# Attention and two feed-forward layers: the first layer's last two blocks by Strassen's algorithm, attention's weights turned in one piece

## The chip, the cores and the metric

The kernel runs on one core of one Trainium2 chip. The metric is the device time of one execution in microseconds. Before the change the median of three runs is 1072.8 us (1071.49 to 1074.07).

## The reference

Three steps follow one another. `q`, `k` and `v` have 4 batches, 8 heads, 768 positions and 64 channels; the output of attention is laid out as 3072 tokens of 512 channels and goes through two feed-forward layers of the same sizes (512 to 2048 to 512).

```python
for c in range(nc):                          # 24 chunks of 32 positions
    k_ctx = k[:, :, max(0, c*32 - 16):min(S, c*32 + 40)]      # v_ctx alike
    k_full = np.concatenate([mem_k, k_ctx], axis=2)           # 8 memory rows
    scores = scale * np.matmul(q_c, k_full.transpose(0, 1, 3, 2))
    a = np.exp(scores - np.max(scores, axis=-1, keepdims=True))
    a = a / (np.sum(a, axis=-1, keepdims=True) + 1e-09)
    out[:, :, c*32:c*32 + 32] = np.matmul(a, v_full)
x = out.transpose(0, 2, 1, 3).reshape(3072, 512)
h = x @ w_in1;  x = np.maximum(0.01 * h, h) @ w_out1          # layer 1
h = x @ w_in2;  x = (h * np.clip(h + 3, 0, 6) / 6) @ w_out2   # layer 2
```

## The kernel before

**Numbers.** A float32 operand of a product is split into a high part, a cast, and a low part, the operand less that cast; a product is then three matmuls (high by high, high by low, low by high) that add up in one bank. ScalarE makes the casts (`high` L902, `cw_high` L884), VectorE or GpSimd the differences (`low` L906, `cw_low` L888).

**Attention.** Two chunks of 32 positions make a "pair" of 64 tokens; there are 48 pairs, 8 to a block of 512 tokens. From pair 16 on (block 2) two pairs go through together, as a double. TensorE makes the scores of one double and the values of the double before in one visit (`visit` L604); VectorE masks and takes the maxima, ScalarE the exponentials, GpSimd the sums and the scaling. VectorE then turns the weights (`a_turn` L541) in blocks of 32x256, twelve to a double, because the value product wants them with the context along the partitions.

**First layer.** Six blocks of 512 tokens, each by 16 units of 128 of the 2048 hidden channels (`hidden` L723 and `output` L748, both through `mm3` L717; their matmuls stand at L719). The weights of this layer are float64 words that are converted once and stay in the core's memory. The attention of a later block lies between the units of an earlier one.

**Second layer.** The blocks go through in three pairs. For a pair of blocks Strassen's scheme (in Winograd's form) replaces eight products of halves by seven: `PROD, LETTERS, FINAL = 7, "BAEBEBD", "ABEAEAD"` (L777) names, product by product, the banks in which the seven products of the hidden half and of the output half add up, and `WIDE` the buffer that holds the split moving operand of each. All of this layer's matmuls stand at L909. Sums on VectorE stand at L899 (operands, `mix`) and L935 (results, `summed`). The weights of this layer are converted piece by piece while the first layer runs (`combine` L1052; `w_clip` L290, `w_join` L297, the quarter sums L840 and L846), stored to DRAM as seven combinations, and loaded into the place of the first layer's weights when that has ended (`cw_load`). The gated hidden values go to DRAM (`g_store`) and come back for the output half (`g_load`), where the split operands use three buffers in turn (`SPIN`: `xwa`, `xwb`, `fb`).

**Order.** The kernel describes every step with an engine, a duration, a due time and what it needs; `Program.order` (L79) runs these steps through a small model of the engines, taking on each free engine the ready step that is due first, and the instructions are then written out in that order. Each engine works through its own list in order. SyncE issues nearly all transfers.

```python
STEP_FIRST = 6.3
STEP_MIXED = 6.6
STEP = 5.5
rings = dict(w=NF - 3, wb=3, raw=2, wa=1, ye=4, g=2, x=4, py=4, ph=2, pa0=1, pa1=1, qk=1, v=1)
def a_turn(pr, part):
    ...
```

Of the kernel before, what the change touches and what calls it, by code (L numbers as in the profile page):

```python
# [23 lines left out]
    visit=1.45, visit2=2.1, scores=0.75, masked=0.56, most=0.55, exp=0.37, exp_all=0.52, small=0.15, inverse=0.18, norm=0.83, turn=0.6, turned=0.57, turn_two=1.35, masked_two=1.1, most_two=0.97,  # L24
# [3 lines left out]
AFTER = 0.1  # L28
LANDING, RATE = 2.1, 290e3
# [4 lines left out]
STEP_MIXED = 6.6  # L34
STEP = 5.5
# [5 lines left out]
LATER = 35.0  # L41


class Program:
# [34 lines left out]
    def order(self, filler):  # L79
# [14 lines left out]
        free_at = {e: 0.0 for e in ready}  # L94
        pipe, out, left, now = 0.0, [], len(steps), 0.0
# [14 lines left out]
        while left:  # L110
            later = []
            for e in free_at:
# [18 lines left out]
                eng, length, _, fn, args, _, takes, nbytes = steps[best]  # L131
                ready[e].discard(best)
# [28 lines left out]
def tile_kernel(  # L161
# [41 lines left out]
    NPB = TB // PT  # L203

# [6 lines left out]

    y_dram = dr.tile([P, KD, NT], F32, tag="yd", name="y_dram")
    w_dram = [dr.tile([P, 7 * NF // 2, 256], F32, tag=f"wd{io}", name=f"w_dram{io}") for io in range(2)]
    g_dram = [dr.tile([P, NB // 2, NF // 2, TB], F32, tag=f"gd{c}", name=f"g_dram{c}") for c in range(4)]
# [5 lines left out]
    aT_all = at.tile([W, 2, HP, P], F32, tag="aT", name="aT_all")  # L220
# [36 lines left out]
    def w_load(layer, f):  # L257
        n = 1 if layer == 0 and f in (0, NF) else 2
        if layer:
            st, src = raw_pair(0).bitcast(U32), (w_in2, w_out2)[f[0]][2 * f[1]:2 * f[1] + 2]  # L260
# [7 lines left out]
    def w_upper(key):  # L268

        raw = raw_t[key][:, :, :, 1].bitcast(F32)  # L270
        if key[0]:
            a = rows(4).bitcast(U32)
# [108 lines left out]
    def barred_by_pe(pr):  # L381
        return pr < 2 * NPB and 0 < pr % PPB < PPB - 1
# [81 lines left out]

    def a_norm_two(pr, k):
# [75 lines left out]
    def a_turn(pr, part):  # L541

        e, t = both(pr), aT_all.rearrange("p k h c -> p (k h) c")
        r = slice(32 * part, 32 * part + 32)
        for j in range(W // 32):
            c = slice(32 * j, 32 * j + 32)
            nc.vector.transpose(out=t[c, :, r], in_=e[r, :, c])  # L547
        if part == P // 32 - 1:
            aT_t[pr], aT_t[pr + 1] = aT_all[:, 0], aT_all[:, 1]
# [8 lines left out]
    def a_turned(pr):  # L558
        t = aT_all[:, pr % 2]
        nc.scalar.copy(out=t.rearrange("p h c -> p (h c)"), in_=aT_t[pr][:W, :])  # L560
# [787 lines left out]
```

## Time and profile before

| | |
|---|---|
| median of three runs | 1072.8 us |
| profiled execution, its own time | 1073.48 us |
| its span in the profile | 1071.7 us |
| TensorE busy | 1058.7 us (99%) |
| VectorE busy | 741.6 us (69%) |
| ScalarE busy | 557.0 us (52%) |
| GpSimd busy | 131.2 us (12%) |
| moved by transfers | 158.35 MB, 148 GB/s over the span |

The span runs from the first to the last instruction of the profiled execution; the execution's own time is 1.8 us longer. "Busy" of TensorE is modelled from the matmuls' ends, so a busy TensorE may still not be at its best pace. The granted clock is 1.00 in every stage read here. The stages, by the products in them: a lead-in to about 33 us, the first layer to about 610 us, the second layer to the end, in it three hidden halves of 76 us to about 834 us and three output halves after that. The busy share of an engine is an average over these; what a change is worth is read stage by stage.

### The profile page before, as it was taken

The numbers are of one execution on the slowest core, as the hardware profiler recorded it, in microseconds if no ns is written. First come the engines' busy times: TensorE is split into PE (matmuls) and PEld (weight loads), VectorE is DVE, ScalarE is ACT, GpSimd is POOL, SyncE is SP. The second block draws the span as 40 slices with busy tenths as digits, with TensorE's granted clock in tenths as the row PEclk, the third lists the DMA queues.
The fourth block names the chain that finished last, engine by engine and source line by source line (L and its number), as shares of the span: only waits on it lengthen the run. The fifth ranks groups of instructions, "written<-read, shape, count | busy, mean of one in ns | idle before, by whom it ended". The sixth has DMA issues, their size and how long they took to land.

```text
span 1071.7 us, 16147 instructions
## 1 busy us (share of the span) xinstructions
PE 1058.7 (99%) x6107; PEld 871.1 (81%) x6107; DVE 741.6 (69%) x1110; ACT 557.0 (52%) x1083; POOL 131.2 (12%) x159
## 2 busy tenths in 40 slices
PE   8999999999999999999999999999999999999997
PEld 7787888888888888888888888888888888888885
DVE  6999856677667766767433666866855796687684
ACT  6887654343435544434344555656677644444442
POOL 4111101100000010000000001111365400000000
PEclk9999999999999999999999999999999999999999
DMA  9564433343345444433433433433677657257313
GB/s 292 194 213 142 158 130 114 113 153 113 128 136 205 138 147 167 139 128 108 155 93 93 140 149 116 154 143 117 207 224 229 229 139 222 49 158 197 64 54 59
DMA packets 101406, 158.35 MB, mean 148 GB/s; under 512 B 32208, under 2 KB 54736, under 8 KB 101328
## 3 DMA queue, kind: packets, MB, share of 16 engines
q1 hardware_dynamic: 101328, 157.32, 45.7%
q8 instruction: 48, 0.79, 0.3%
q14 instruction: 30, 0.25, 0.1%
HBM read 104.86 MB, written 52.43 MB: 147 GB/s over the span
## 4 chain that ended last, share of the span: by engine, by line
PE 95%; DMA 2%; DVE 1%; ACT 1%; SPq 0%; issue 0%; DVEq 0%
PE ph L719 25%; PE py L719 25%; PE sA L909 12%; PE sE L909 12%; PE sB L909 12%; PE sD L909 6%; PE px L568 2%; PE psc L404 2%; DMA in<-in_v_dram 1%; DMA f<-in_moe_w_dram 1%; DMA cw<-w_dram 1%; PE psc L568 0%; PE pt L555 0%; SPq L369 0%; DVE a L304 0%
## 5 line engine op out<-in xcount | busy, mean ns | idle before, releaser
L719 PE MATMUL py<-g,w 128*128 128x512 f32 x1152 | 279.5, 390 | 0.0
L719 PE MATMUL ph<-xh,w 128*128 128x512 f32 x768 | 258.4, 394 | 0.7 <-ACT xh L584 0.7
L719 PEld LDWEIGHTS py<-g,w 128*128 128x128 f32 x1152 | 215.2, 188 | 45.0 <-DVE g L746 0.2
L719 PEld LDWEIGHTS ph<-xh,w 128*128 128x128 f32 x768 | 144.9, 189 | 31.9 <-ACT xh L584 0.9
L737 ACT ACTIVATE ph<-ph 128x512 f32<-128x512 f32 x96 | 56.0, 583 | 189.6 <-PE ph L719 185.3
L719 PE MATMUL ph<-xl,w 128*128 128x512 f32 x384 | 150.3, 391 | 0.0
L746 DVE TENSOR_TENSOR g<-ph,g 128x512 fp32r<-128x512 f32 x96 | 66.2, 689 | 96.3 <-ACT g L741 95.7
L547 DVE STREAM_TRANSPOSE aT_all<-raw 32x256 f32<-32x256 f32 x192 | 83.4, 435 | 4.5 <-POOL raw L468 1.8
L719 PEld LDWEIGHTS ph<-xl,w 128*128 128x128 f32 x384 | 72.5, 189 | 14.7 <-DVE xl L590 0.3
L945 POOL TENSOR_TENSOR gated<-gated,gated 128x512 f32<-128x512 f32 x24 | 33.8, 1419 | 245.7 <-PE sB L909 130.1
L741 ACT CAST g<-ph 128x512 fp32r<-128x512 f32 x96 | 56.4, 588 | 2.9
L909 PE MATMUL sE<-xwb,cw 128*128 128x512 f32 x240 | 57.6, 389 | 0.0
L531 POOL TENSOR_SCALAR su<-su 128x4 f32<-128x4 f32 (+1 forms) x32 | 9.9, 309 | 368.7 <-ACT raw L461 331.5
L909 PEld LDWEIGHTS sE<-xwb,cw 128*128 128x128 f32 x240 | 45.0, 188 | 9.4
L584 ACT CAST xh<-px 128x512 fp32r<-128x512 f32 (+1 forms) x25 | 12.8, 512 | 71.5 <-PE px L568 71.5
L461 ACT ACTIVATE raw<-raw,mx 128x96 f32<-128x96 f32 x128 | 46.2, 365 | 3.3 <-DVE mx L457 3.3
L909 PE MATMUL sB<-fb,cw 128*128 128x512 f32 x192 | 46.6, 390 | 0.4 <-DVE gated L942 0.4
L909 PE MATMUL sB<-xwa,cw 128*128 128x512 f32 x192 | 46.1, 389 | 0.0
L935 DVE TENSOR_TENSOR sE<-sE,small_ye 128x512 f32<-128x512 f32 x24 | 16.8, 698 | 38.8 <-PE sE L909 38.2
L909 PEld LDWEIGHTS sB<-fb,cw 128*128 128x128 f32 x192 | 36.0, 188 | 8.3 <-DVE gated L942 0.8
L909 PEld LDWEIGHTS sB<-xwa,cw 128*128 128x128 f32 x192 | 36.0, 188 | 7.5
L888 POOL TENSOR_TENSOR cw<-cw 128x512 fp32r<-128x512 f32 x28 | 37.9, 1364 | 33.8 <-ACT cw L884 29.4
(158 smaller groups left out, 1853.8 us busy)
## 6 DMA issues: line engine op xcount, KB each, us to landing
g_dram<-gated SPq DMA_DIRECT2D x96, 256.0 KB, 2.0
f<-in_moe_w_dram SPq DMA_DIRECT2D x15, 1024.0 KB, 5.0
cw<-w_dram SPq DMA_DIRECT2D x56, 256.0 KB, 3.1
raw<-g_dram SPq DMA_DIRECT2D x24, 512.0 KB, 4.0
raw<-in_moe_w_in_dram SPq DMA_DIRECT2D x8, 1024.0 KB, 5.8
w_dram<-raw SPq DMA_DIRECT2D x32, 256.0 KB, 2.3
raw<-in_moe_w_out_dram SPq DMA_DIRECT2D x8, 1024.0 KB, 5.2
qk_now<-in_qk_dram SPq DMA_DIRECT2D x24, 320.0 KB, 4.1
```

The source lines that it names most:

```text
L404: nc.tensor.matmul(pt[j][n * PT:(n + 1) * PT, m * W:(m + 1) * W], qt[r, hp, :], kt[r, hp, :], start=not more, stop=True, tile_position=(e ...
L461: nc.scalar.activation(out=e[:, k, :], in_=e[:, k, :], func=AF.Exp, bias=m_t[pr][:, k:k + 1], accum_out=s_t[pr][:, k:k + 1],)
L547: nc.vector.transpose(out=t[c, :, r], in_=e[r, :, c])
L568: nc.tensor.matmul(pt[e * D:(e + 1) * D, at + hp * every:at + hp * every + PT], vt[:, c], t[:, hp, n * PT:(n + 1) * PT], start=True, stop= ...
L719: nc.tensor.matmul(dst, a, b, start=first and i == 0, stop=last and i == len(terms) - 1)
L737: nc.scalar.activation(out=ph, in_=ph, func=AF.Prelu, alpha=0.01)
L741: nc.scalar.copy(out=g[:, 0, :], in_=ph_t[key])
L746: nc.vector.tensor_sub(out=g[:, 1, :], in0=ph, in1=g[:, 0, :].bitcast(F32))
L888: eng.tensor_tensor(out=w[:, :, 1, :], in0=w[:, :, 1, :].bitcast(F32), in1=w[:, :, 0, :].bitcast(F32), op=ALU.subtract)
L909: nc.tensor.matmul(dst, a, b, start=start, stop=True, skip_group_check=True)
L935: nc.vector.tensor_tensor(out=t if out else b, in0=b, in1=t, op=ALU.add)
L945: nc.gpsimd.tensor_tensor(out=gated(a), in0=gated(b), in1=gated(a), op=ALU.subtract)
```

## The change

The first four blocks of the first layer stay as they were. Its last two go through the same seven-product scheme as the second layer's pairs. For that the attention of these two blocks is written to DRAM (`x_staged`, `x_store`) and loaded back as operands. The first layer's weights, which are held as high and low parts, are added up again (`c_whole`), combined in quarters like the second layer's, and stored; the seven combinations are then streamed back in units of four blocks and split again on VectorE. The hidden values pass a leaky rectifier on ScalarE alone (`rectify`), and the results go to `y_dram`. From here on this stretch is the inserted pair.

Attention of blocks 2 to 5 is packed between the products of blocks 1 to 3. Its weights are turned by one instruction for a double, in 32x32 blocks in place, and the blocks are brought to their partitions by a store to DRAM and three loads. The value products stand two visits behind the scores.

```diff
-    def a_turn(pr, part):
+    def a_turn(pr):
 
-        e, t = both(pr), aT_all.rearrange("p k h c -> p (k h) c")
-        r = slice(32 * part, 32 * part + 32)
-        for j in range(W // 32):
-            c = slice(32 * j, 32 * j + 32)
-            nc.vector.transpose(out=t[c, :, r], in_=e[r, :, c])
...
+        nc.vector.transpose(out=turned_t, in_=both(pr).rearrange("p h (j c) -> p j h c", c=32))
+
+    def turn_store(pr):
+        nc.sync.dma_start(out=turn_dram[pr // 2 % 2], in_=turned_t.rearrange("p j h c -> p j (h c)"))
+
+    def turn_load(pr, j):
+        nc.sync.dma_start(
+            out=aT_all[32 * j:32 * j + 32].rearrange("i r h c -> i r (h c)"),
+            in_=turn_dram[pr // 2 % 2].rearrange("(r i) j x -> i r j x", i=32)[:, :, j, :],
+        )
...
-                    pt[e * D:(e + 1) * D, at + hp * every:at + hp * every + PT], vt[:, c], t[:, hp, n * PT:(n + 1) * PT],
+                    pt[e * D:(e + 1) * D, at + hp * every:at + hp * every + PT].rearrange("p (r c) -> p r c", c=32),
+                    vt[:, c], t[:, 2 * n:2 * n + 2, hp, :],
...
+    def c_whole(key, e):
...
+        w = wt[0, 2 * p + e, io]
+        nc.vector.tensor_tensor(out=rows(4)[:, e, :], in0=w[:, 0, :].bitcast(F32), in1=w[:, 1, :].bitcast(F32), op=ALU.add)
...
-    def cw_load(io, t):
-        nc.sync.dma_start(out=combined(t)[:, :, 1, :].bitcast(F32), in_=w_dram[io][:, 2 * t:2 * t + 2, :])
+    def cw_load(y, io, u):
+        nc.sync.dma_start(out=combined(y, io, u)[:, :, 1, :].bitcast(F32), in_=w_dram[y][io][:, 4 * u:4 * u + 4, :])
...
+    def rectify(letter, k, n):
+        nc.scalar.activation(out=gated(n), in_=sums(letter, k), func=AF.Prelu, alpha=0.01)
...
+    def y_store(blk, c, n):
+        nc.sync.dma_start(out=y_dram[:, c, blk * TB:(blk + 1) * TB], in_=small(n))
...
-    for blk in range(NB):
+    for blk in range(CB):
         block_at[0, blk] = t
-        length[0, blk] = STEP if blk == NB - 1 else STEP_MIXED if blk else STEP_FIRST
+        length[0, blk] = STEP_MIXED if blk else STEP_FIRST
         t += NF * length[0, blk]
...
-    first = block_at[0, 1] + 25
-    every = (block_at[0, NB - 1] - 25 - first) / 16
+    first, end = block_at[0, 1] + 6, hidden_at[0, 0] - 30
     for n in range(16):
-        combine(n % 8, n // 8, first + n * every)
+        combine_first(n % 8, n // 8, first + n * (end - first) / 16)
+    stages = [first, hidden_at[0, 0], output_at[0, 0], *(hidden_at[1, s] for s in range(NS)), output_at[1, 0] - 25]
+    for n, t, u in zip((W0, W1, W2, W3, W4, 16 - W0 - W1 - W2 - W3 - W4), stages, stages[1:]):
+        combine_between(n, t, u)
...
-    WIDE = ["fb8", "x0", "x1", "xwa", "xwb", "x2", "x3"]
-    SPIN = ["xwa", "xwb", "fb8"]
+    WIDE = [["fb8", "x0", "x1", "xwa", "xwb", "x2", "x3"], ["x0", "x1", "xwa", "xwb", "fb8", "x2", "x3"]]
+    SPIN = ["fb8", "xwa", "xwb"]
...
+        if y == 0:
+            cell("ACT", T["relu"], t, rectify, letter, k, n, reads=b, writes=g, **gated_own(n))
+            return n
...
+        for u in range(UNITS):
+            add_weights(y, 1, u, output_at[y, 0] + u * 4 * H6 - 20, "POOL" if y else "DVE")
```

With `CLASSICAL = 4` there are four blocks in the loop over `CB`. `W0` to `W4` (9, 1, 0, 1, 3, and 2 left over) say in which stage the sixteen conversions of second-layer weights lie: nine beside the first layer's blocks, one in the hidden half of the inserted pair, six in the second layer's hidden halves.

**How the order moves.** The rows below are an engine's instructions as they stand one after the other; they hold no times. Names with a number at their end are buffers: `fb8`, `xwa`, `xwb` the split operands, `ob` and `ot` reloaded hidden values, `cw` combined weights, `cv` and `cva` the second layer's weights in conversion.

VectorE in an output half, from the end of the second product on, before (the second layer's first output half):

```order
L906 TENSOR_TENSOR xwb_5587<-ob1_7223,xwb_5587 128x1024
L906 TENSOR_TENSOR fb8_4949<-ot0_7226,fb8_4949 128x1024
L899 TENSOR_TENSOR ot0_7226<-ot0_7226,raw1_1554 128x1024
L899 TENSOR_TENSOR ob0_7115<-ob0_7115,ot0_7226 128x1024
L906 TENSOR_TENSOR xwa_5542<-ot0_7226,xwa_5542 128x1024
L935 TENSOR_TENSOR wa_1834<-sB0_5523,wa_1834 128x512
```

and in the output half of the inserted pair:

```order
L330 ISA cva_1702<-cv_1642,cva_1702 128x2048
L1030 TENSOR_TENSOR fb8_4414<-ob1_0_5072,fb8_4414 128x1024
L956 TENSOR_TENSOR cv_1642<-cva_1702 128x256
L962 TENSOR_TENSOR cv_1642<-cva_1702 128x256
L962 TENSOR_TENSOR cv_1642<-cv_1642,cva_1702 128x256
L962 TENSOR_TENSOR cv_1642<-cva_1702,cv_1642 128x256
L1030 TENSOR_TENSOR xwb_4542<-ot0_0_5076,xwb_4542 128x1024
L1022 TENSOR_TENSOR ot0_0_5076<-ot0_0_5076,raw1_1543 128x1024
L1022 TENSOR_TENSOR ob0_0_4970<-ob0_0_4970,ot0_0_5076 128x1024
L1005 TENSOR_TENSOR cw1_10_5108<-cw1_10_5108 128x4x256
L1030 TENSOR_TENSOR xwa_4529<-ob1_0_5072,xwa_4529 128x1024
```

The split of `ot0` now stands ahead of the last split of `ob1`, a conversion of second-layer weights lies between the splits, and so does a split of combined weights (`cw1_10`), which GpSimd made before.

TensorE at the same place, before (from the last rows of the second product on):

```order
L909 MATMUL sB0_5523<-xwb_5587,cw3_5139 128x512 x3
L909 MATMUL sB1_5535<-xwb_5587,cw3_5139 128x512 x3
...
L909 MATMUL sE0_5593<-fb8_4949,cw4_5175 128x512 x3
L909 MATMUL sE1_5607<-fb8_4949,cw4_5175 128x512 x3
...
```

and in the inserted pair:

```order
L1033 MATMUL sB0_4462<-fb8_4414,cw1_3_4755 128x512 x3
L1033 MATMUL sB1_4475<-fb8_4414,cw1_3_4755 128x512 x3
...
L1033 MATMUL sE0_4522<-xwb_4542,cw1_4_4791 128x512 x3
L1033 MATMUL sE1_4533<-xwb_4542,cw1_4_4791 128x512 x3
...
L1033 MATMUL sB0_4462<-xwa_4529,cw1_3_4755 128x512 x3
L1033 MATMUL sB1_4475<-xwa_4529,cw1_3_4755 128x512 x3
...
```

The first four products of E (from `xwb`) have moved ahead of the last four of B (from `xwa`).

VectorE around the first product of the second layer, before:

```order
L746 TENSOR_TENSOR g0_5_15_5519<-ph0_5_15_5487,g0_5_15_5519 128x512
L906 TENSOR_TENSOR xwa_5542<-raw1_1554,xwa_5542 128x1024
L899 TENSOR_TENSOR raw1_1554<-raw0_1774,raw1_1554 128x1024
L935 TENSOR_TENSOR sA0_5546<-sA0_5546,wa_1834 128x512
L762 COPY yo5_0_5574<-py0_5_0_5005 128x512
```

and now:

```order
L1060 TENSOR_TENSOR small_ye2_4628<-sD0_4545,small_ye2_4628 128x512
L1022 TENSOR_TENSOR raw0_1658<-raw1_1543,raw0_1658 128x1024
L1060 TENSOR_TENSOR small_ye3_4638<-sD1_4589,small_ye3_4638 128x512
L312 TENSOR_SCALAR cva_1702<-cva_1702 128x1024
L1060 TENSOR_TENSOR sA0_4497<-sA0_4497,wa_1644 128x512
L1030 TENSOR_TENSOR xwa_4529<-raw0_1658,xwa_4529 128x1024
L1022 TENSOR_TENSOR raw0_1658<-raw0_1658 128x1024
L1022 TENSOR_TENSOR raw1_1543<-raw1_1543,raw0_1658 128x1024
L1060 TENSOR_TENSOR sA1_4510<-sA1_4510,wa_1644 128x512
L1030 TENSOR_TENSOR xwb_4542<-raw0_1658,xwb_4542 128x1024
```

The last result sums of the inserted pair and the sums of operands and of the next hidden values now stand in one row ahead of `xwa` and `xwb`, with a conversion step (L312) among them.

## Rows read from the trace of the kernel before

**Rows 1.** The page: busy time, share of the span, instructions of each engine.

```profile
PE 1058.7 (99%) x6107; PEld 871.1 (81%) x6107; DVE 741.6 (69%) x1110; ACT 557.0 (52%) x1083; POOL 131.2 (12%) x159
```

**Rows 2.** The page: the chain that ended last, by engine.

```profile
PE 95%; DMA 2%; DVE 1%; ACT 1%; SPq 0%; issue 0%; DVEq 0%
```

**Rows 3.** Waits of TensorE from 33 us on: us in total, times, longest.

```profile
PE ph L719 <- ACT xh L584: 0.7, 1, 0.7
PE sB L909 <- DVE gated L942: 0.4, 1, 0.4
```

**Rows 4.** Windows: from, to, length, then busy time (instructions) of each engine.

```profile
core 0: us, PE busy (x) PEld busy (x) DVE busy (x) ACT busy (x) POOL busy (x), PEclk, DMA share, GB/s
...
134.00:520.00 386.00, 386.00 (x2549) 317.58 (x2549) 262.49 (x481) 169.84 (x442) 32.61 (x48) 1.00 0.41 139
...
760.00:830.00 70.00, 69.64 (x308) 57.30 (x307) 43.87 (x62) 50.14 (x85) 40.69 (x30) 1.00 0.72 232
772.00:776.00 4.00, 4.00 (x20) 3.30 (x19) 1.78 (x3) 2.46 (x6) 2.33 (x2) 1.00 0.97 359
776.00:780.00 4.00, 3.63 (x16) 2.70 (x15) 3.84 (x8) 3.45 (x6) 1.44 (x2) 1.00 0.99 352
912.00:988.00 76.00, 76.00 (x337) 62.94 (x336) 56.56 (x57) 33.68 (x36) 0.00 (x0) 1.00 0.51 139
```

**Rows 5.** Windows, line 719 on TensorE alone: the first layer's products.

```profile
33.00:1072.00 1039.00, 533.93 (x2304) 1.00 0.45 144
```

**Rows 6.** Windows, line 909 on TensorE alone: the second layer's products.

```profile
570.00:1072.00 502.00, 457.62 (x2016) 1.00 0.47 145
```

**Rows 7.** Timeline of TensorE in the last products: start, length, instruction, count.

```profile
1053.20 2.88 PE L909 MATMUL sD<-fb,cw 128*128 128x512 f32 x12
1055.92 2.88 PE L909 MATMUL sD<-xwa,cw 128*128 128x512 f32 x12
```

**Rows 8.** Timeline of TensorE over one attention visit.

```profile
42.38 0.56 PE L404 MATMUL psc<-qk_now 64*64 64x96 f32 x16
42.87 0.69 PE L568 MATMUL psc<-aT_all,v_now 96*64 96x64 f32 x16
43.48 0.73 PE L719 MATMUL py<-g,w 128*128 128x512 f32 x2
```

**Rows 9.** Timeline of VectorE in an output half, instructions back to back.

```profile
1023.72 1.22 DVE L906 TENSOR_TENSOR xwb<-ot,xwb 128x1024 fp32r<-128x1024 f32 x1
1024.85 1.21 DVE L906 TENSOR_TENSOR fb<-ot,fb 128x1024 fp32r<-128x1024 f32 x1
1025.99 1.22 DVE L899 TENSOR_TENSOR ob<-ob,ot 128x1024 f32<-128x1024 f32 x1
```

**Rows 10.** Timeline of ScalarE there: a cast that waited for a buffer.

```profile
1039.80 1.05 ACT L902 CAST fb<-ot 128x1024 fp32r<-128x1024 f32 x1 [1.67 <-PE sE L909]
```

**Rows 11.** Groups of VectorE by form: count, busy, mean ns, idle before.

```profile
L547 DVE STREAM_TRANSPOSE aT_all<-raw 32x256 f32<-32x256 f32 x192 | 83.4, 435 | 4.5 <-POOL raw L468 1.8
L297 DVE SCALAR_TENSOR_TENSOR wa<-raw,wa 128x1024 uint32<-128x1024 uint32 x16 | 19.5, 1220 | 0.4
L935 DVE TENSOR_TENSOR sE<-sE,small_ye 128x512 f32<-128x512 f32 x24 | 16.8, 698 | 38.8 <-PE sE L909 38.2 <-issue 0.6
L290 DVE TENSOR_SCALAR wa<-wa 128x1024 uint32<-128x1024 uint32 x16 | 11.6, 725 | 0.5
L955 DVE STREAM_TRANSPOSE gated<-small_ye 128x512 f32<-128x512 f32 x12 | 7.8, 685 | 0.0
L846 DVE TENSOR_TENSOR raw<-raw,wa 128x256 f32<-128x256 f32 x16 | 7.3, 454 | 0.4
```

**Rows 12.** Timeline of VectorE over one double: masking, then half its turns.

```profile
249.46 1.02 DVE L438 SCALAR_TENSOR_TENSOR raw<-psc,masks 128x384 f32<-128x384 f32 x2 [1.39 <-PE psc L404]
259.42 2.67 DVE L547 STREAM_TRANSPOSE aT_all<-raw 32x256 f32<-32x256 f32 x6
```

More of the change, by code (lines that the diff above doesn't have):

```diff
@@ L40 @@
 COLD = 5.5
-LATER = 35.0
+LATER = 10.0
+CLASSICAL = 4
+LATEST = 0.0
+W0 = 9
+W1 = 1
+W2 = 0
+W3 = 1
+W4 = 3
+PACE = 17.5
+LAST_STEP = 13.0
+SPREAD = 3.4
+BY_ACT = 0
+DEEP = 1
 class Program:
@@ new lines, in sums_of @@
+    def sums_of(key, u, m, w, **more):
+        y, (io, p) = key
+        cell("DVE", T["quarter"], u - 1, c_first, key, reads=[w], writes=[m])
+        for n in range(3):
+            c = cell("DVE", T["quarter"], u - 0.5 + 0.5 * n, c_more, key, n, reads=[w], writes=[m])
+        c_stored[y, io, p] = []
+        for n in range(4):
+            c_stored[y, io, p].append(
+                cell("SP", T["load"], u + 1.5 + 0.5 * n, c_store, key, n, reads=[m] if n > 1 else [w],
+                     nbytes=P * (1024 if n == 1 - io else 2048), **more)
+            )
@@ new lines, in combine_first @@
+    def combine_first(p, io, u):
+        key, m, w = (0, (io, p)), ("raw", 2), ("wide", 0)
+        hold = [max((x for x in paced if x[0] <= u - 10))[1]]
+        u += LATER
+        for e in range(2):
+            f = 2 * p + e
+            cell("DVE", T["sum"], u - 2.5 + 0.7 * e, c_whole, key, e, after=[w_ready[0, f, io], *hold], writes=[w],
+                 takes=takes_early(), frees=[(tag_of(f), ("u", f))])
+        sums_of(key, u, m, w)
+        early.extend(c_stored[0, io, p])
+    taken_early = []
@@ L1102, in wide_own @@
             used[c] = True
-            return dict(takes=[("wb" if c == "xwb" else "w", c)])
-        return own("x", c)
+            return dict(takes=[("wb", c)])
+        return own("x", f"{c}_{y}")
     def bank_own(letter, k):
@@ new lines, in tile_kernel, with add_weights @@
+    SPIN = ["fb8", "xwa", "xwb"]
+    UNITS = PROD * NQ // 4
+    def add_weights(y, io, u, need, eng):
+        stage = ("L", 0) if y else ("S", io)
+        w = [("cw", stage, u)]
+        pairs = {n // PROD if io == 0 else n % NQ for n in range(4 * u, 4 * u + 4)}
+        owned = own(cw_tag(y, u), ("cw", stage, u))
+        taken["w"] = cell("SP", T["load"], need - 24, cw_load, y, io, u, writes=w, nbytes=P * 4096,
+                           **merged(owned, dict(after=[x for p in sorted(pairs) for x in c_stored[y, io, p]] + [taken.get("w")])))
+        cell("ACT", T["wide_copy"], need - 9, cw_high, y, io, u, writes=w)
+        if eng == "DVE":
+            cell("DVE", T["wide"], need - 8, cw_low, y, io, u, nc.vector, writes=w)
+        else:
+            cell("POOL", 2 * T["pool"], need - 8, cw_low, y, io, u, nc.gpsimd, writes=w)
@@ L1219, in load, with mixed @@
                     if dst[0] == "x":
-                        more = own("x", f"o{dst[1]}{w // 2}")
-                    cell("SP", T["load"], due, g_load, c, s, w, dst, writes=[dst], nbytes=P * 4096,
-                         **merged(more, dict(after=[g_stored[c, s, 2 * w + e] for e in range(2)])))
-                def mixed(dst, x, y, op):
-                    cell("DVE", T["wide"], need - 5.4, mix, dst, x, y, op, reads=[x, y], writes=[dst])
+                        more = own("x", f"o{dst[2]}{w // 2}_{y}")
+                    taken["x"] = cell("SP", T["load"], due, g_load, y, c, s, w, dst, writes=[dst], nbytes=P * 4096,
+                         **merged(more, dict(after=[g_stored[y, c, s, 2 * w + e] for e in range(2)])))
+                def mixed(dst, x, z, op):
+                    cell("DVE", T["wide"], need - 5.4, mix, dst, x, z, op, reads=[x, z], writes=[dst])
                 c = SPIN[spun[0] % 3]
```

511 lines of the change are left out of this document (311 added, 200 removed).

## The prediction, made before the changed kernel had run

> **What bounds the kernel now.** I read four views in this order. The page's busy line comes first: TensorE is busy 1058.7 us of 1071.7 us, and VectorE, the next, 741.6 us [rows 1]. A share alone can mislead, so the chain of work that ended last comes second: 95% of it is TensorE [rows 2]. Third, the waits of TensorE after the lead-in: two in 1039 us, 0.7 and 0.4 us [rows 3]. Fourth, the stages: from 134 to 520 us TensorE is busy 386.00 of 386.00 us while VectorE has 262 us of work, and in an output half of the second layer it is busy 76.00 of 76 us beside 56.6 us of VectorE [rows 4]. So only two things move the end: the number of products on TensorE, and a wait that a slower helper puts in front of one.
>
> A product is a matmul of 128x128 by 512 columns. Twelve of them start 2.72 us after the twelve before [rows 7], so one costs 0.2267 us, whatever the 0.39 us in which the profile draws each. That pitch is the price I use, not the busy time.
>
> **The change part by part.**
>
> *Products.* The first layer has 2304 products [rows 5], 384 for each of its six blocks of 512 tokens; two blocks are 768, or 174.1 us. The second layer has 2016 [rows 6], 672 for each pair of blocks, by the same seven-product scheme that the last pair of the first layer now gets: 152.3 us. The difference, 96 products at 0.2267 us, is **-21.8 us**, all of it on the path. I call the new 152.3 us the inserted pair: its hidden half ends at T1, its output half at T2, 76.2 us each.
>
> *Attention on TensorE.* Scores, turns and values are as many as before; they are packed into three blocks instead of four. Sixteen score matmuls start 0.49 us before the next sort, sixteen value matmuls 0.61 us [rows 8]. New is that a value matmul reads its 64 columns in two runs of 32. No row shows that. Below, it cannot gain: the columns are the same. Above, I let a second run cost what separates the two sorts, 0.0075 us, for 768 matmuls: 5.8 us. The time of a matmul here does not follow its columns (96 take less than 64), so I take 0.
>
> *Attention on VectorE.* 192 small transposes, 83.4 us, go [rows 11]. Sixteen of 768 columns come; the nearest rows are 0.435 us for 256 columns and 0.685 us for 512, so about 0.93 us each, 15 us. None of the 68 us saved is on the path, since TensorE lost nothing there [rows 4]; it pays for the new weight sums. What is late next is the road through DRAM: one store and three loads of 128 KB. From the masking to the transposes a double of pairs now takes 10 us [rows 12]; with the turn and two trips of some 3 us that is 17 us. The value products stand two visits behind the scores. Sixteen visits share three blocks, 261 us of products, so two visits are over 32 us. The products between hide it: 0.
>
> *Weights of the first layer.* Thirty-two sums that rebuild a unit, 64 quarter sums and 28 splits of 1024 columns are new on VectorE. In blocks two to four VectorE's rows come to some 68 us per block by the durations before, while a block's products alone take 87 us; the stretch from 134 to 520 us has 262 us in 386 now [rows 4], the same share or a little less. Cost 0; without the products over it, it would be all of those 60 us.
>
> *Output half of the inserted pair.* Here VectorE is closest to the limit. Between T1 and T2 its order holds 27 splits of a moving operand, 13 sums, 11 splits of weights, 8 result sums and one conversion of second-layer weights. Back-to-back instructions of 1024 columns start 1.135 us apart, though each lasts 1.22 us [rows 9]: 51 x 1.135 = 57.9. The result sums are 8 x 0.69 = 5.5, the conversion 2 x 0.72 + 2 x 1.22 + 4 x 0.44 = 5.6 [rows 11]. Together 69 of 76 us, against 56.6 before. An in-order queue this full waits somewhere, and the order shows where. Three buffers hold the split operand, so a split starts when the product three back has ended, plus 0.2 us and a cast of 1.06 us on ScalarE [rows 10]. The sixth split starts at T1 + 3 x 2.72 + 1.3 = 9.4; the conversion's first four rows stand behind it, so the seventh starts at 14.1; the quarter sums and the wait for its buffer put the split of ot0 at 17.6; two sums and cw1_10 follow, so xwa from ob1 starts at 22.15 and is done at 23.4. TensorE, which takes E before the last B, wants it after eight products, at 21.8. It waits **1.7 us**. Later splits meet their product with 0.1 us or more to spare in the same count. Bounds: 0, if loads let the order run ahead, and 8 us, if half of the 15 us more work that this half has than one before lands on TensorE.
>
> *Start of the second layer.* In the old kernel it stands behind products that need few splits. Now VectorE reaches T2 with the last result sums still to do. By its order: sum, mix, sum, shift, then sA0 (which needs TensorE's third unit, T2 + 4.3), then xwa, done at 6.1. TensorE has put five units of 1.36 us before it, 6.8. xwb is done at 10.1 against 10.9. So 0, with 0.7 us to spare. Bounds 0 and 3 us (both splits late by a conversion step of 1.2 us).
>
> *Hand-overs.* Three are new: into the inserted pair, from its hidden to its output half (same tokens, so stored values come back at once), and out of it. The only such place now cost 0.4 us [rows 3, 4]. 3 x 0.4 = **1.2 us**; bounds 0 and 6.
>
> *Six conversions* move into the second layer's hidden halves. A bank is wanted again 4.1 us after its last product, and sum, gate and second gate need about 2.4; one instruction of 1.14 us in front still fits. 0; at most 6 x 1.1 us.
>
> *Lead-in.* Its loads come in another order; I take 0, within 1 us either way.
>
> **Sum.** The profiled execution took 1073.5 us (span 1071.7). 1073.5 - 21.8 + 1.7 + 1.2 = 1054.6 us. The median of the runs, 1072.8, lies 0.7 us lower: **1054 us**.
>
> **Rivals.**
>
> *Transfers bind the inserted pair.* From its first store to the second layer's last row load SyncE issues 106 transfers: stored and reloaded values 16.8 MB, weights 13.6, rows of x and y 6.8, conversions 5.9, together 43.1 MB in 152.3 us, 283 GB/s. For it: from 760 to 830 us the rate was 232 GB/s at a share of 0.72. Against it: that stretch was not full, and full ones reach 352 to 359 GB/s at 0.97 to 0.99 [rows 4]. At 232 GB/s the pair would take 185.8 us, and the time would be 1054 + 33.5 = 1087 us. It turns slower than before when the rate falls below 43.1 / (152.3 + 18.9), 252 GB/s. The Trainium skill (DMA: Bandwidth & Descriptors, section Bandwidth) speaks for this rival: it asks for transfers of 1 MiB and lists 138 GB/s at 64 KB and 341 at 1 MB; between them I estimate some 265 GB/s for transfers of 256 and 512 KB, and the time by that would be about 1064 us. The rows of 352 to 359 GB/s were reached with transfers of 256 and 512 KB, several at once, and they decide. Chance 0.10, of which 0.03 past the turning point.
>
> *VectorE binds the output half.* If the instructions do not overlap (1.22 instead of 1.135 us), its 51 long ones cost 4.3 us more, the half no longer fits with its waits, and those 4.3 us reach TensorE: 1058 us. For it: mixed neighbours on several buffers, and splits that come 0.1 us ahead of their product. Against it: rows 9 are the same instructions. The Trainium skill (VectorE: DVE Perf Modes, section The DRAIN you can't avoid) says the next operation does not start before the pipe is empty, which would be this case; the trace does not agree, with starts 1.13 us apart for operations of 1.22 us. Chance 0.13.
>
> *The turned weights come late (slower).* If the road through DRAM outlasts two visits, TensorE stands still at every one of 16 value visits. From 1.2 us each the saving of 18.9 us is gone; at 2 us it is 1054 + 32 = 1086 us. For it: the transfers stand in SyncE's one queue behind stores that wait for VectorE. Against it: 17 us of work in over 32. Chance 0.07, half of it past the turning point.
>
> **How the numbers follow.** The forecast has 0.70. Its own edges are 1050 (no wait and a lead-in 1 us shorter) and 1060 (5.8 us for the column runs). To leave at most 2 in 10 outside I take in VectorE's case, the mild part of the transfers, and 12 us, nearly half, of the upper bounds above (6.3 + 3 + 4.8 + 5.8 + 6.6 = 26.5 us beyond the values taken): 1050 to 1066. Within 0.2% of before, 2.1 us, counts as no change; that is about what a measurement of this kernel can tell. Slower: 0.03 + 0.03; no change 0.02 between; faster 0.92.
>
> **What would show it.** Right: 4224 products at 0.2267 us; blocks two to four with no wait of TensorE; VectorE near 69 of 76 us in the output half, and one wait of 1 to 2 us on a split into xwa early in it. Wrong: a stretch of the inserted pair with the transfers' share near 1 and TensorE waiting for loads; value products waiting for aT_all; or a wait of over 2 us behind the first xwa of the second layer.

## The result, and the profile after

The changed kernel takes 1055.09 us (median of four runs, 1054.41 to 1055.60) against 1072.14 us of the kernel before in the same comparison: a ratio of 0.9839, 95% interval 0.9828 to 0.9851. The forecast was 1054 us with a range of 1050 to 1066. The profiled execution took 1054.41 us, its span is 1052.6 us.

The page's busy line [rows 1]: TensorE is still busy nearly all the time, VectorE has risen from 69% to 77%.

```profile
PE 1036.0 (98%) x5992; PEld 850.9 (81%) x5992; DVE 811.8 (77%) x1091; ACT 615.5 (58%) x1122; POOL 152.8 (15%) x153
```

Windows with the first layer's classical products alone, and with the products of the seven-product scheme alone [rows 5, 6]: 1536 and 2688, which is 4224 in place of 4320.

```profile
28.00:1054.00 1026.00, 358.01 (x1536) 1.00 0.65 209
28.00:1054.00 1026.00, 610.24 (x2688) 1.00 0.65 209
```

The timeline of TensorE near the end [rows 7]: twelve products still start 2.72 us after the twelve before.

```profile
1033.99 2.88 PE L1033 MATMUL sD<-fb,cw 128*128 128x512 f32 x12
1036.71 2.88 PE L1033 MATMUL sD<-xwa,cw 128*128 128x512 f32 x12
```

The waits of TensorE from 33 us on (total, times, longest) [rows 3]. The first is the one forecast; the third lies in the second layer's first output half; the others are in attention between the units of block zero. None is on a load, none on turned weights of blocks two to five. (`xwa`, `xwb` and `fb` are buffers of split operands; `sA` to `sE` are banks of TensorE's results.)

```profile
PE sB L1033 <- DVE xwa L1030: 1.5, 1, 1.5
PE psc L421 <- ACT aT_all L594: 1.4, 2, 0.7
PE sE L1033 <- DVE xwb L1030: 0.9, 1, 0.9
PE psc L430 <- ACT aT_all L594: 0.7, 1, 0.7
PE pt L589 <- POOL e L569: 0.2, 1, 0.2
```

Windows [rows 4]: the stretch of the classical blocks and the inserted hidden half, then the inserted pair's two halves, then an output half of the second layer. In the inserted output half VectorE works 70.25 of 78 us.

```profile
core 0: us, PE busy (x) PEld busy (x) DVE busy (x) ACT busy (x) POOL busy (x), PEclk, DMA share, GB/s
134.00:520.00 386.00, 386.00 (x2549) 317.42 (x2548) 267.04 (x410) 212.88 (x503) 47.66 (x56) 1.00 0.79 259
...
430.90:508.50 77.60, 77.60 (x344) 64.23 (x344) 60.34 (x73) 56.28 (x86) 9.28 (x6) 1.00 0.81 269
508.50:586.50 78.00, 76.47 (x338) 63.00 (x337) 70.25 (x69) 50.16 (x55) 2.54 (x2) 1.00 0.79 265
...
892.00:968.00 76.00, 76.00 (x337) 62.93 (x336) 56.58 (x57) 33.72 (x36) 0.00 (x0) 1.00 0.52 139
```

The timeline of VectorE in that half, around the conversion of second-layer weights (L312 to L962). From 518.2 to 532.3 us, where the late split ends, no gap is over 0.3 us:

```profile
518.19 1.23 DVE L1030 TENSOR_TENSOR xwb<-ob,xwb 128x1024 fp32r<-128x1024 f32 x1 [1.54 <-ACT xwb L1026]
519.33 0.69 DVE L312 TENSOR_SCALAR cva<-cva 128x1024 f32<-128x1024 f32 x1
...
523.28 1.22 DVE L1030 TENSOR_TENSOR fb<-ob,fb 128x1024 fp32r<-128x1024 f32 x1
...
526.31 1.22 DVE L1030 TENSOR_TENSOR xwb<-ot,xwb 128x1024 fp32r<-128x1024 f32 x1 [0.21 <-ACT xwb L1026]
...
529.97 1.22 DVE L1005 TENSOR_TENSOR cw<-cw 128x1024 fp32r<-128x1024 f32 x1
531.10 1.22 DVE L1030 TENSOR_TENSOR xwa<-ob,xwa 128x1024 fp32r<-128x1024 f32 x1
532.24 1.22 DVE L1030 TENSOR_TENSOR fb<-ot,fb 128x1024 fp32r<-128x1024 f32 x1
```

And the timeline of TensorE there: eight times 2.72 us after this half began (at 508.7 us) it wants `xwa`, which is ready at 532.3.

```profile
527.74 2.88 PE L1033 MATMUL sE<-xwb,cw 128*128 128x512 f32 x12
530.46 0.39 PE L1033 MATMUL sB<-xwa,cw 128*128 128x512 f32 x1
532.38 1.89 PE L1033 MATMUL sB<-xwa,cw 128*128 128x512 f32 x7 [1.53 <-DVE xwa L1030]
```

### The profile page after: what moved, and what is told of

The parts are those of the page before. It is cut to its first block, busy times and chain, and to the rows that moved or that the text cites. A ratio compares the mean times of both kernels' runs of the same rounds, so it can differ in the third digit from the quotient of the medians.

```text
span 1052.6 us, 16284 instructions
## 1 busy us (share of the span) xinstructions
PE 1036.0 (98%) x5992; PEld 850.9 (81%) x5992; DVE 811.8 (77%) x1091; ACT 615.5 (58%) x1122; POOL 152.8 (15%) x153
## 5 line engine op out<-in xcount | busy, mean ns | idle before, releaser
L823 PE MATMUL py<-g,w 128*128 128x512 f32 x768 | 187.7, 392 | 0.0
L823 PE MATMUL ph<-xh,w 128*128 128x512 f32 x512 | 170.5, 393 | 0.0
L823 PEld LDWEIGHTS py<-g,w 128*128 128x128 f32 x768 | 142.8, 188 | 30.3 <-DVE g L850 0.4
L1033 PE MATMUL sB<-x,cw 128*128 128x512 f32 x336 | 81.5, 389 | 0.0
L1033 PEld LDWEIGHTS sB<-x,cw 128*128 128x128 f32 x336 | 63.1, 188 | 13.1
L1033 PE MATMUL sE<-xwa,cw 128*128 128x512 f32 x276 | 66.3, 389 | 0.0
L1033 PE MATMUL sE<-fb,cw 128*128 128x512 f32 x264 | 63.4, 389 | 0.0
L1001 ACT CAST cw<-cw 128x1024 fp32r<-128x1024 f32 x56 | 58.7, 1053 | 6.1 <-DMA cw<-w_dram 6.1
L1033 PEld LDWEIGHTS sE<-xwa,cw 128*128 128x128 f32 x276 | 51.8, 188 | 10.8
L1005 DVE TENSOR_TENSOR cw<-cw 128x1024 fp32r<-128x1024 f32 x42 | 51.8, 1245 | 7.2 <-ACT cw L1001 7.2
L561 POOL TENSOR_SCALAR su<-su 128x4 f32<-128x4 f32 (+1 forms) x32 | 12.4, 389 | 269.3 <-ACT raw L487 219.7
```

Source lines behind the costliest of these rows:

```text
L561: nc.gpsimd.tensor_scalar_add(su, su, 1e-9)
L823: nc.tensor.matmul(dst, a, b, start=first and i == 0, stop=last and i == len(terms) - 1)
L1001: nc.scalar.copy(out=w[:, :, 0, :], in_=w[:, :, 1, :].bitcast(F32))
L1005: eng.tensor_tensor(out=w[:, :, 1, :], in0=w[:, :, 1, :].bitcast(F32), in1=w[:, :, 0, :].bitcast(F32), op=ALU.subtract)
L1033: nc.tensor.matmul(dst, a, b, start=start, stop=True, skip_group_check=True)
```

## The experiments

My theory: TensorE is the bound, so the saving is the 96 products; VectorE stands close behind it in the inserted output half, where one conversion too many makes the 1.5 us wait; the turned weights and the transfers are covered. The rivals are those of the prediction. The name in brackets behind a heading is the run's. Each expectation below was on record before its run. A half's length is measured from its first product to the first product of the next half. Ratios are to the kernel before; the changed kernel's is 0.9839.

**No conversion among the splits** (no_conv). The twelfth conversion waits for the inserted pair's first result.

```diff
+HELD = 11
...
-        cell("SP", T["load"], t - 9, w_load, 1, (io, p), after=hold, writes=r, nbytes=P * 8192)
+        a = cell("SP", T["load"], t - 9, w_load, 1, (io, p), after=hold, writes=r, nbytes=P * 8192)
+        loads.append(a)
...
+    program.steps[loads[HELD]][5].append(evicted[CB + 1, 0])
```

> The changed kernel, with its twelfth conversion of second-layer weights held back until the inserted pair's first result is stored, so that no conversion lies among VectorE's splits in that output half. My theory (VectorE's in-order queue is too full there, and the conversion's 5.6 us stand ahead of the late split): the wait of TensorE on the split into xwa (1.5 us now) is gone or under 0.3 us, VectorE is busy 63 to 65 of 76 us there, and the time falls by 1.5 us to about 1053.6. Rival (the wait comes from the buffers' order, since products take E before the last B): the wait stays within 0.3 us of 1.5 and the time is unchanged. Second rival: the fifth conversion in the second layer's hidden half brings a wait of its own of about 1 us there, and the time stays at 1055.

1069.06 us, ratio 0.9972 (0.9960 to 0.9984). The wait is gone as expected: the inserted output half takes 76.2 us, with VectorE busy 64 us. But the time rises. The second rival came in place, at more than its price: two of the second layer's hidden halves take 77.3 and 78.8 us instead of 76.2, the latter with a wait of 2.3 us. The largest loss lies where no expectation had put it: the second layer's first output half takes 89.2 us instead of 77.4. (Another 3.8 us of this execution lie before the first layer's 385th product, where the order is still the changed kernel's; they are not the edit's.) The windows of the two output halves, and that of a stretch after a wait:

```profile
512.30:588.40 76.10, 76.10 (x337) 63.04 (x336) 64.13 (x61) 49.73 (x54) 2.54 (x2) 1.00 0.75 251
820.60:909.90 89.30, 81.62 (x338) 65.90 (x338) 78.78 (x59) 44.81 (x49) 35.42 (x13) 0.94 0.69 206
871.00:877.00 6.00, 5.15 (x12) 4.13 (x13) 4.21 (x4) 1.33 (x2) 0.00 (x0) 0.50 0.29 87
```

GpSimd is busy 35.4 us in that half (18.3 in the changed kernel): the late conversion has made the loads of combined weights late (the last goes out at 858 us instead of 824), and GpSimd's splits of them, which in the changed kernel end at 842 us, now go on to 871 us, beside VectorE's splits. Timelines of both engines at 857 us:

```profile
857.35 3.36 DVE L1031 TENSOR_TENSOR xwb<-ot,xwb 128x1024 fp32r<-128x1024 f32 x1
...
861.77 3.39 DVE L1023 TENSOR_TENSOR ot<-ot,raw 128x1024 f32<-128x1024 f32 x1
```

```profile
856.73 2.90 POOL L1006 TENSOR_TENSOR cw<-cw 128x1024 fp32r<-128x1024 f32 x1 [0.38 <-ACT cw L1002]
860.62 3.46 POOL L1006 TENSOR_TENSOR cw<-cw 128x1024 fp32r<-128x1024 f32 x1 [0.99 <-ACT cw L1002]
```

An instruction of VectorE that lasts 1.22 us elsewhere lasts 3.4, and each ends 1.08 us after GpSimd's (859.63 and 860.71; 864.08 and 865.16). So the two do not share, they take turns. The Trainium skill (SBUF — State Buffer, section SBUF: two separate sides) says so: an operation of VectorE with two operands in this memory and one of GpSimd hold a common pair of ports in turn, each for its whole length; the trace agrees.

**GpSimd for the splits in the inserted output half** (pool).

```diff
-            add_weights(y, 1, u, output_at[y, 0] + u * 4 * H6 - 20, "POOL" if y else "DVE")
+            add_weights(y, 1, u, output_at[y, 0] + u * 4 * H6 - 20, "POOL")
```

> The changed kernel with the splits of combined weights in the inserted output half on GpSimd (fourteen, 2.4 us each) instead of VectorE (1.135 us each). By counts alone VectorE has 14 x 1.135 = 16 us less to do and TensorE's wait of 1.5 us goes: 1053.5 us (rival: GpSimd is free help). My theory, from the kernel with the held conversion, where VectorE's instructions of 1024 columns last 3.4 instead of 1.2 us while GpSimd splits weights: each such split costs VectorE about 2.2 us, 31 us in all against 16 saved, VectorE comes to some 85 us in a half of 76, and the half takes 4 to 12 us longer than 78: 1059 to 1067 us.

1066.79 us, ratio 0.9955 (0.9941 to 0.9969). The total is as I expected, but not for my reason alone: the inserted output half takes 79.9 us (78.0 before), 1.9 us more where I had said 4 to 12, with VectorE busy 74.8 us (not 85) although it has fourteen splits fewer to do. Most of the loss, 9.2 us, is again in the second layer's first output half (86.6 us), where this order's conversions also come later (the last at 792 us, at 760 in the changed kernel); 3.0 us of the profiled execution lie before the 385th product, where the order is unchanged. In the inserted half itself GpSimd is no free help beside VectorE.

**Conversions earlier instead of later** (early_p). Eleven beside the classical blocks, none in the inserted output half, four left for the second layer as in the changed kernel.

```diff
-W0 = 9
+W0 = 11
...
-W4 = 3
+W4 = 2
...
+HELD = 12
...
+    program.steps[loads[HELD]][5].append(evicted[CB + 1, 0])
```

> The changed kernel with eleven conversions of second-layer weights planned beside the first layer's blocks instead of nine, and the thirteenth held back until the inserted pair's first result is stored: twelve are done before the inserted pair's output half, none lies in it, and four are left for the second layer's hidden halves, as in the changed kernel. My theory (the conversion ahead of the late split is the cause of the wait in the inserted output half, and holding it back cost 14 us only because the work landed on the start of the second layer's first output half): the inserted output half takes 76.2 us instead of 78.0, the second layer's first output half stays at 77.4 or below, and the time is 1053.3. Rival (any shift of these conversions upsets the second layer's output half): that half takes 80 us or more, and the time is 1057 or more.

1055.95 us, ratio 0.9850 (0.9836 to 0.9863): no gain. Both halves do what was expected (76.2 and 77.3 us), but the inserted hidden half takes 80.0 us instead of 77.5, with two new waits, 1.2 us behind a copy on ScalarE and 0.6 on a split. The wait has moved one half ahead; the rival fell, and so did my 1053.3.

**The planner's model as before** (old_model). In the changed kernel attention between the units of block zero has 2.3 us of waits, which the kernel before does not have.

```diff
-    visit=1.45, visit2=2.1, scores2=1.3, values2=1.1, scores=0.75, masked=0.56, most=0.55, exp=0.37, exp_all=0.52, small=0.15, inverse=0.18, norm=0.72, turn=0.6, turned=0.57, turn_two=1.0, masked_two=1.1, most_two=0.97,
+    visit=1.45, visit2=2.1, scores2=1.3, values2=1.1, scores=0.75, masked=0.56, most=0.55, exp=0.37, exp_all=0.52, small=0.15, inverse=0.18, norm=0.83, turn=0.6, turned=0.57, turn_two=1.0, masked_two=1.1, most_two=0.97,
...
-SHARED = {"w_clip", "w_shift", "w_join", "w_add", "w_low", "cw_low", "c_whole", "c_first", "c_more", "mix", "low", "a_norm", "a_norm_two", "g_differ"}
+SHARED = set()
```

> The changed kernel with the planner's model as before: no shared port, and 0.83 us instead of 0.72 for the scaling of attention's weights. Up to the end of block one the order is then that of the kernel before. My theory (the 2.5 us earlier first product and the 2.9 us of new waits on attention's turns in block one both come from these two lines): first product at 32.6 us, no such waits after it, and 1.1 us less on the first product's low part: in sum about -1.5 us up to the end of block one. Rival (the later stages need the port model): waits of TensorE in the inserted pair grow by 2 us or more, and the time is 1056 or more.

1053.73 us, ratio 0.9834 (0.9821 to 0.9847). The median is 1.4 us under the changed kernel's, where I had said 1.5, but the kernel before took 1071.49 us beside it and 1072.14 beside the changed kernel; by the ratios the two differ by 0.5 us, which is within their intervals. The trace shows the parts: the waits at block zero fall from 2.3 to 0.4 us, and the first layer's 385th product starts at 136.0 us instead of 138.0, though the first one starts at 31.9 and not at 32.6. The rival is right in its sign but not in its size: waits in the inserted output half rise from 1.5 to 2.7 us (79.8 us for the half instead of 78.0), and the time stays under its 1056. Waits from 33 us on:

```profile
PE sE L1033 <- DVE fb L1030: 1.7, 1, 1.7
PE sB L1033 <- DVE xwa L1030: 1.0, 2, 0.6
PE pt L589 <- POOL e L569: 0.4, 1, 0.4
```

**Both together** (early_o), the edits for earlier conversions and for the old model, and then once more (early_o2) beside the changed kernel (after_same) on one chip:

> The same with the planner's model as before (no shared port, 0.83 us for the scaling), that is with the changes of early_p and of old_model together. If the two causes add up: old_model's 1053.7 us less the 3.6 us by which its inserted output half (79.8) is over 76.2 us: 1050.1. Rival: without the port model GpSimd's and VectorE's work fall on each other and the waits move on: 1053 or more.

> The changed kernel itself, beside the next one on the same chip: 1055 us.

> The kernel early_o itself (conversions earlier, planner's model as before), beside the changed kernel on the same chip. If removed waits are time: the changed kernel's profile has 1.5 + 0.9 us of waits in output halves and 2.1 us at attention in block one that early_o's lacks, early_o's has 1.0 us that the changed kernel lacks: 3 us shorter in all, ratio to it 0.997. Rival: the two medians told apart only the chips (1055.1 and 1053.4 in two jobs): ratio 1.000.

1053.40 us, ratio 0.9830 (0.9816 to 0.9843); beside each other 1053.69 (0.9819, 0.9798 to 0.9841) against 1054.86 us (0.9829, 0.9809 to 0.9850). The gains do not add up to 1050.1 (the rival said 1053 or more), and 1.2 us between the two (a ratio of 0.999, between my 0.997 and the rival's 1.000) is less than their intervals: a version that is clearly better was not found. From 33 us on the traces of early_o and early_o2 list no wait over 0.9 us, and each of the orders tried here made waits that the others lack.

**The old turn in the changed kernel** (old_turn). Twelve small transposes per double, value products one visit behind.

```diff
-        program.cell("DVE", T["turn_two"], due(5.2), a_turn, d, reads=E, writes=U)
-        w = program.cell("SP", T["load"], due(5.5), turn_store, d, reads=U, writes=D, nbytes=P * 3072)
...
+        for i in range(P // 32):
+            c = program.cell("DVE", 1.35, due(5.6 + 0.3 * i), a_turn, d, i, reads=E, writes=[("aT", 0), ("aT", 1)])
```

> The changed kernel with the twelve small transposes per double of the kernel before in place of the one long transpose, the store and the three loads; value products one visit behind the scores. VectorE has 83 us instead of 16 us of transposes in blocks two to four, some 22 us more for each 96 us: 88 of 96. My theory (the new weight sums live on the room that the one-piece turn makes): queues that full make TensorE wait, 3 to 15 us in all, so 1058 to 1070 us. Rival (the products hide this too, since TensorE's waits begin only where VectorE is full): under 1 us of waits, 1055 us, and the turn part of the change is worth nothing.

1071.37 us, ratio 0.9995 (0.9986 to 1.0004): without the new turn the whole gain is gone, a little beyond my 3 to 15 us. VectorE is busy 83.8, 87.5 and 84.2 us in the stretches of 96 us where the changed kernel has 66.0, 63.5 and 64.5. The loss is not mainly there: the first layer's blocks lose some 5 us, and the second layer's first output half takes 87.5 us, where the pattern is that of no_conv: the conversions slide back (the last at 793 us), GpSimd's splits end at 871 us again, and VectorE's instructions beside them last up to 3.4 us.

**The turn alone in the kernel before** (turn_only2). Value products one visit behind, as there. The edit is that of `a_turn`, `turn_store` and `turn_load` above; to make room for the new buffer it also sets `dynamic_dma_scratch_size=1024`, as the changed kernel does, and what that does by itself was not tried.

> The kernel before with the turn alone: one transpose per double, a store and three loads, six blocks classical, value products one visit behind. My theory (68 us of VectorE's time off the path are worth nothing while TensorE never waits there): 1072 us, within 2 us, and no wait of TensorE on turned weights, since a visit comes every 24 us and the road takes about 17. Rival (the road through DRAM is late): TensorE waits on the turned weights at 16 visits, 1 us each or more, 1088 us or more.

1092.17 us, ratio 1.0188 (1.0175 to 1.0202): I was wrong, the rival is right in sign, though at 2 of 16 visits and not at all of them (waits of 7.5 and 3.0 us on turned weights; behind them the granted clock is 0.50 for 10.2 and 6.8 us, and each is followed by a wait of 0.7 us on the next product's operand). The timelines of SyncE and TensorE show the road:

```profile
322.28 0.33 SPq L548 DMA_DIRECT2D turn_dram<-turned  x1
...
326.03 0.43 SPq L551 DMA_DIRECT2D aT_all<-turn_dram  x1
...
331.42 0.50 SPq L551 DMA_DIRECT2D aT_all<-turn_dram  x1
```

```profile
334.66 1.12 PE L576 MATMUL px<-aT_all,v_now 96*64 96x64 f32 x16 [7.47 <-DMA aT_all<-turn_dram]
```

The masking began at 311.5, the transpose ended at 322.3, and the three loads went out at 326.0, 329.5 and 331.4, between stores of results and weights in SyncE's one queue: 23 us from masking to value product where I had counted 17.

**One visit behind in the changed kernel** (one_behind).

```diff
-DEEP = 1
+DEEP = 0
...
-        attention_two(d, queue.pop(0) if n != 1 else None, at0 + PACE * n, SPREAD)
+        attention_two(d, queue.pop(0), at0 + PACE * n, SPREAD)
...
```

> The changed kernel with the value products one visit behind the scores instead of two, and the turned weights loaded at once; all else alike. In the changed kernel the road from a score visit to the landing of the turned weights takes some 19 us (visit at 163, transpose ended at 175, loads landing 4 us after their issue), and visits come every 17.1 us. My theory (the two visits are what hides the road): visits are drawn apart to 19 us or more, sixteen of them take over 300 us where three blocks of products give some 290, and TensorE waits 10 to 40 us on loads of turned weights: 1065 to 1095 us. Rival (the order finds other products to put ahead of a late visit): no wait over 1 us on turned weights, 1055 to 1057 us.

1103.73 us, ratio 1.0292 (1.0276 to 1.0309). The stretch from the first product to the inserted pair grows from 400.9 to 443.0 us; four waits on turned weights are 25.2 us, the longest 13.1, and the granted clock is 0.50 for 41 us around them. So it is the second visit that hides the road, and without it the change is 31 us slower than the kernel before.

**Two matmuls in place of three** (two_terms) in every product of the inserted pair; its results lose the low part of the weights.

```diff
-            mm(dst, wl, xh[:, k, :], False)
+            if y:
+                mm(dst, wl, xh[:, k, :], False)
```

(the same in `o_product`)

> The changed kernel without the low-by-high matmul of every product of the inserted pair (448 instead of 672 of a half; the results of that pair lose their low weight part). By products alone each half takes 50.8 us less 25.4, that is 50.8 instead of 76.2, and the time is 1004 us. My theory (VectorE is close behind TensorE there): the halves end where VectorE is full, at its busy time of now: 60 to 66 us for the hidden half, 69 to 74 us for the output half: about 1055 - 13 - 6 = 1036 us, within 8 us, with VectorE busy 95% or more of the output half. Rival (VectorE waits rather than works there): the halves come to 55 us or less and the time is under 1015.

1040.99 us, ratio 0.9708 (0.9689 to 0.9728). With a third of the products gone the halves take 67.3 and 72.5 us instead of 50.8 each; VectorE is busy 71.3 of 74 us in the window of the output half:

```profile
431.00:498.00 67.00, 57.34 (x230) 44.30 (x229) 55.55 (x68) 52.59 (x82) 9.66 (x6) 0.95 0.87 284
498.00:572.00 74.00, 58.11 (x232) 43.49 (x231) 71.25 (x71) 52.41 (x61) 2.56 (x2) 0.98 0.85 293
```

So in the output half VectorE's bound lies 3.7 us under TensorE's 76.2, as my theory has it. The hidden half is held at 67, 1 us over what I expected, and by something else: the largest waits there are 6.5 us on ScalarE's gates.

**More bytes** (more_bytes). A copy in DRAM of each unit beside its load, 14.7 MB.

```diff
+        if y == 0:
+            nc.sync.dma_start(out=w_copy[io][:, 4 * u:4 * u + 4, :], in_=w_dram[y][io][:, 4 * u:4 * u + 4, :])
```

> The changed kernel with a copy in DRAM of each unit of combined weights beside its load in the inserted pair: 28 transfers of 512 KB, 14.7 MB more within some 155 us (95 GB/s on top of the 264 to 270 GB/s that the two halves show at a share of 0.78 to 0.81). My theory (transfers have a reserve of about a fifth there): the share comes to 0.95 or more, loads come late at places, and the pair takes 3 to 15 us longer: 1058 to 1070 us. Rival (the loads are issued so far ahead that this hides too): 1055 to 1056 us at a share of 0.95 or more. Second rival (the transfers bound the pair already): the pair stretches by the bytes, 14.7 MB at 270 GB/s, over 40 us.

1058.59 us, ratio 0.9880 (0.9864 to 0.9897); the profiled execution's span is 1054.5 us, 1.9 over the changed kernel's. The inserted pair's window:

```profile
431.00:586.00 155.00, 152.98 (x674) 126.04 (x673) 129.80 (x139) 107.25 (x143) 11.80 (x8) 1.00 0.92 326
```

326 GB/s instead of 267, and the waits of TensorE in the pair grow by 0.5 us: the 267 GB/s were what the pair asks for, not what the transfers can give. The median is at the low edge of what I expected, but not as I expected it: of the 1.9 us in the profiled execution the pair has 0.8, and 0.7 are a wait on turned weights at 403 us, ahead of it. That execution is the fastest of four (1056.31 to 1061.19), and where the slower ones lose more was not read.

## Why the prediction was right

The forecast was -18.9 us on the profiled execution's own time; it fell from 1073.48 to 1054.41, by 19.1. The medians differ by 17.05, where 1072.8 to 1054 would be 18.8: the profiled execution of the kernel before was slower than its median, that of the changed kernel faster. By its steps:

- *Products*, -21.8: right. Number and pitch are as counted; old_turn and one_behind show that the count alone gives nothing when VectorE or the road is late.
- *The wait in the inserted output half*, +1.7: right, in place and size. The late split of `xwa` was to start 22.15 us after the half began and started 22.4 after; TensorE waited 1.5, and the half is 1.8 us longer than the 76.2 of its products. VectorE was to work 69 us and worked 70.25. (The upper bound of 8 us was mis-sized: it takes 15 us of work more than in a half before, where the prediction's own 69 and 56.6 make it 12.4.) That the conversion makes the wait is shown by its absence in no_conv and early_p.
- *Hand-overs*, +1.2: wrong by all of it. No product waits at 431.2, 508.7 or 586.7 us.
- *Start of the second layer*, 0: right, no wait on its splits.
- *Attention on TensorE*, 0: right. The turned weights in two runs of 32 columns cost nothing (the first value row is 0.51 us ahead of the next, as in the kernel before). The first two rows are from before, the last two from the changed kernel:

```profile
249.36 0.69 PE L568 MATMUL px<-aT_all,v_now 96*64 96x64 f32 x16
249.87 0.64 PE L568 MATMUL px<-aT_all,raw 96*64 96x64 f32 x16
...
180.21 0.69 PE L604 MATMUL px<-aT_all,v_now 96*64 96x64 f32 x16
180.72 0.64 PE L604 MATMUL px<-aT_all,raw 96*64 96x64 f32 x16
```

- *Attention on VectorE*: the long transpose lasts 0.97 us (0.93 estimated), and the cover of two visits holds. My 17 us for the road was too short (23 us in turn_only2); its margin came from the second visit.
- *Weights of the first layer*, 0: right. VectorE is busy 64 to 66 us per 96, forecast 68.
- *Six conversions in the hidden halves*: the trace shows four (at 636, 690, 710 and 760 us); two more ran ahead of their stage. No wait came of them, but their real risk, GpSimd's splits sliding onto an output half, was not among my rivals; in three experiments it is the largest loss.
- *Lead-in*, 0 within 1 us: missed for the first product, right for what follows. The first product starts at 30.3 us instead of 32.9, but the first layer's 385th product starts at 138.0 us instead of 137.9, with the same work on TensorE in between: new waits, 1.1 us on the first product's low part and 2.3 us at block zero, which were not in the sum, eat the gain. On the other side the granted clock of the kernel before is not 1.00 in every stage, as its description above has it, but 0.57 from 33 to 37 us, which is worth about 1 us by old_model (its first 32 products take 10.2 us, those of the kernel before 11.2):

```profile
32.85 0.50 PE L719 MATMUL ph<-xh,w 128*128 128x512 f32 x1 [0.72 <-ACT xh L584]
33.00:37.00 4.00, 4.00 (x10) 2.98 (x11) 3.85 (x6) 3.31 (x10) 1.46 (x3) 0.57 1.02 392
...
30.30 0.50 PE L823 MATMUL ph<-xh,w 128*128 128x512 f32 x1
31.93 0.50 PE L823 MATMUL ph<-xl,w 128*128 128x512 f32 x1 [1.13 <-DVE xl L636]
```

  The earlier start goes with the new order and not with this execution alone: with the changed kernel's order up to there the first product starts at 29.9 to 30.8 us in seven traces, with the order before at 31.7 to 32.9 in five. The two exceptions are no_conv and pool (32.9 and 32.8): in their lead-in the granted clock is 0.50 for 6.8 and 3.4 us from 17 us on, as in none of the seven; what brought it down was not tried.
- *Not in the sum* behind the 385th product: the wait in the second layer's first output half makes it 1.2 us longer than its products, where the kernel before has 0.7 us in a hidden half. So -21.8 + 1.8 + 1.2 - 0.7 + 0.1 = -19.4; the spans' difference is -19.1. That the forecast of the profiled execution came within 0.2 us is in part luck: the hand-overs that did not come (1.2 us) stand against waits that it did not name.

The rivals: transfers do not bind (more_bytes). VectorE does not bind the output half at three matmuls, but is within 4 us of it (two_terms), and its instructions of 1024 columns still start 1.13 us apart (529.97, 531.10, 532.24 us). The Trainium skill (VectorE: DVE Perf Modes, section The DRAIN you can't avoid) does not speak against such rows, as the prediction has it: the same paragraph says that a next operation that is not held starts earlier. The turned weights would have come late with one visit less (one_behind, turn_only2).

## What to carry to other kernels

When one engine is busy without a gap, price a change by the work it takes off that engine, and then go through the next busy engine's queue in order, instruction by instruction: that found the wait in the inserted output half to 0.2 us. Work that is taken off an engine with room to spare need not save anything by itself: the turn alone made the kernel before slower, since its road was late (turn_only2), but without it the whole gain is gone (old_turn), since it makes the room that the saving needs. A small step that is delayed is not priced where it stands, but where the work behind it lands (no_conv).

## What the runs showed of the hardware

- VectorE and GpSimd take turns on operands in the core's memory: instructions of 1.22 us last 3.4 us beside GpSimd's splits (no_conv), and each ends 1.08 us after GpSimd's has ended.
- A wait of TensorE can cost more than its length. After 3.85 us without a product the granted clock is 0.50, the level of 1.2 GHz, and products start 0.427 us apart instead of 0.227 for the next 5 us (no_conv, its timeline of TensorE; the window from 871 us above). After the 1.5 us wait of the changed kernel the clock stayed at 1.00; in pool, after waits of 1.5 and 2.0 us with one product between them, it was 0.50 for 6.8 us. The first two rows are no_conv's, the last two pool's.

```profile
871.85 5.06 PE L1034 MATMUL sA<-xwa,cw 128*128 128x512 f32 x11 [3.85 <-DVE xwa L1031]
876.71 1.54 PE L1034 MATMUL sE<-xwb,cw 128*128 128x512 f32 x4
...
858.34 0.50 PE L1033 MATMUL sA<-xwb,cw 128*128 128x512 f32 x1 [1.48 <-ACT xwb L1026]
860.86 5.06 PE L1033 MATMUL sA<-xwb,cw 128*128 128x512 f32 x11 [2.02 <-DVE xwb L1030]
```
